# Denominators on two scratch tiles, key work from GpSimd to VectorE and ScalarE, and chunks of 256, 256 and seven times 512 tokens

## The chip, the core and the metric

The kernel runs on one core of a Trainium2 chip. The metric is the time of one execution in microseconds (us), taken on the device. The core's engines work side by side, each through its own queue in the order of the program, and wait for one another through semaphores: TensorE (PE in the rows; PEld is its loading of weights) multiplies, VectorE (DVE) and ScalarE (ACT) work on single elements, GpSimd (POOL) does the same more slowly, and SyncE (SP) issues transfers. SBUF is the core's memory for operands, PSUM the one that TensorE writes.

## What is computed

The first half is attention with random features, for 8 batches of 576 tokens and 8 heads of 64 dimensions, 128 features (M). The second half is a layer of 512 to 2048 and back to 512 columns on all 4608 tokens:

```python
def phi(x):                       # x is q or k, scaled
    proj = np.einsum('bhsd,md->bhsm', x, omega)
    sq = np.sum(x * x, axis=-1, keepdims=True) / 2.0
    h = proj - sq
    h = h - np.max(h, axis=-1, keepdims=True)
    return np.exp(h) / np.sqrt(m)
q_p, k_p = (phi(q_s), phi(k_s))
kv = np.einsum('bhsm,bhsd->bhmd', k_p, v)
z = np.sum(k_p, axis=2)
num = np.einsum('bhsm,bhmd->bhsd', q_p, kv)
den = np.einsum('bhsm,bhm->bhs', q_p, z)[..., None] + 1e-06
attn = num / den
# x: attn with heads side by side, (4608, 512)
h = x @ w_in
out = (h - np.tanh(h)) @ w_out
```

## The kernel before

The products run in a rounded 32-bit format (F32R). To keep the precision of 32 bits, an operand is split into a high part (the rounded value) and a low part (the rest), and two or three products take the place of one.

The tokens are cut into chunks of `SIZE = [256, 256, 256, 384, 384, 512, ...]` (chunks 0 and 1 are worked as one of 512). The program has two lists of steps. `ORDER` is the start: it decodes the weights, and does the keys of batches 0 to 2 and the queries of chunks 0 and 1. `LATER` holds all the rest, written as tokens `unit.step.slot`, and each engine's queue gets its instructions in just this order. Units are:

- `k` + batch + pair of heads (`k_unit`): the keys. Steps `p`, `c`, `t`, `e` make the features (project, copy out of PSUM, row minimum, exponential) for five groups of tokens, A0, A1, M, B0 and B1; head A has groups A0 and A1, head B has B0 and B1, and M is the last 64 tokens of either head, one head on partitions 0 to 63 and the other on 64 to 127. `kh`/`kl` split the features (`khl`), `vh`/`vl` the values (`vhl`), `kv` multiplies them into `pk`. `zA`, `zB`, `zM` sum the features over tokens into `zs`, `zh`/`zl` split the sum, and `ca` to `wv` turn and split the result, `kvw`, with `zb` the sum spread over all partitions.
- `q` + chunk + pair (`q_unit`): the queries. The same steps `p` to `e` for each tile of 128 tokens, then `d` (denominators: for each tile, head and batch one `tensor_tensor_reduce` on DVE, whose product goes to a scratch tile `junk` and whose sum goes to `dn`), `n` (reciprocal and division), `z`, `a`, `l` (turn and split), `m` (numerators), `ta`, `tv`, `xh`, `xl` (into the layer's input).
- `f` + chunk + slice of 128 columns of the 2048 (`f_unit`): the layer. `h0`, `h1` are 12 products on TensorE, `th` is tanh on ScalarE, `g` a subtraction on DVE (line 759), `gh` (ScalarE) and `gl` (DVE) the split, `o0` to `o3` the products with `w_out`. A unit of a chunk of 256 tokens takes two slices at once and is 512 columns wide on DVE and ScalarE, one of a chunk of 384 is 384 wide. `s` units copy out and send.

In a key unit GpSimd does the low parts of the features (line 646), the high parts of the values (659, with zeros set for group M at 656 and 657), the sums (680, 681, 685, 686) and the low part of `zs` (693). DVE does the rest of the element work beside ScalarE. Group M's values are split on 64 partitions at a time, one operation for each head (664).

Of the kernel before, what the change touches and what calls it, by code (L numbers as in the profile page):

```python
# [89 lines left out]
s0.c2.1 f21.h0.6 s0.c3.0 s0.d2 q30.n1 s0.d3 q31.t0 f21.h1 q31.t1 q31.e0 q31.t2 q31.e1 q32.sv q30.z0.0 q31.e2 k30.pA0.4  # L90
k30.pA1.7 q31.d0 f21.th q33.ld f20.o0.2 q30.a0 q31.d1 k30.cA0.0 k30.cA1 f21.g f20.o1.3 q30.l0 f21.gh q31.d2 k30.pM.0
f21.gl f22.h0.6 k30.cM.0 q31.n0 q31.n1 f22.h1 k30.tA0 k30.tA1 k30.eA0 k30.tM k30.vlA1 k30.eA1 q30.m0.4 k30.khA0.0
f21.o0 f22.th k30.klA0 k30.khA1.1 q30.ta0.2 f22.g k30.klA1 k30.eM f21.o1 q30.tv0 f22.gh k30.zA.0 f22.gl q30.z1.7
f23.h0.6 q30.a1 q30.l1 f23.h1 q30.m1.0 f23.th q32.p0.4 q32.p1.7 q30.ta1 f23.g f22.o0 q32.c0.0 q32.c1 q30.tv1 f23.gh
q32.t0 f22.o1 f23.gl q32.e0 q32.t1 q32.d0 q32.e1 q31.z0.0 q32.p2.4 q31.a0 q32.d1 k30.pB0.7 f24.h0.6 q32.c2 q33.sa
q31.l0 q32.t2 k30.cB0.0 q33.sv f24.h1 q32.e2 q32.d2 q40.ld q31.m0.0 q32.n0 f24.th k30.pB1.4 f23.o0 q31.ta0.3 q32.n1
k30.cB1 f24.g k31.sa q31.tv0 f23.o1 k30.tB0 f24.gh k30.tB1 k30.eB0 f24.gl q31.z1.0 k30.eB1 k30.kvA0.7 k31.sv0 k30.kvA1
q31.a1 k30.vhM.0 q33.p0.4 k30.khM.0 f25.h0.6 k30.khB0.1 q33.c0.1 q31.l1 k30.klM q33.t0 k30.klB0 k30.vlM q33.e0 f25.h1
k31.sv1 k30.zB.0 q33.d0 k32.ld q31.m1.0 f25.th k30.zM q33.p1.4 k30.kvM q31.ta1 f25.g f24.o0 q33.c1 k30.vhB0.0 q31.tv1
f25.gh k30.vhB1.1 q33.t1 f24.o1 f25.gl q33.e1 k30.khB1.0 q33.d1 k30.klB1 q32.z0.0 k30.vlB0 q33.p2.4 k30.vlB1 q32.a0  # L100
f26.h0.6 k31.lv q33.c2 q32.l0 q40.sa q33.t2 f26.h1 q33.e2 q40.sv q33.d2 q41.ld q32.m0.0 f26.th q33.n0 k30.kvB0 k30.kvB1
q32.ta0.1 k31.vhA0.0 q32.z1.4 f26.g k30.ca.0 f25.o0 k31.vhA1.1 q32.a1 q32.tv0 f26.gh q32.l1 f26.gl f25.o1 q33.n1
k30.zh.0 k30.cv q32.m1.0 k30.zl k31.vlA0 q40.p0.4 k31.vlA1 q32.ta1 f27.h0.6 q40.c0.0 q32.tv1 q40.t0 f27.h1 q40.e0
q30.xh q40.d0 q31.xh q33.z0.0 q30.xl f27.th q40.p1.4 q31.xl k30.kt q32.xh f27.g f26.o0 q33.a0 q40.c1 q32.xl f27.gh
q33.l0 k30.ka k30.zb f26.o1 f27.gl q40.t1 k30.kb q40.e1 q33.m0.0 q40.p2.4 k30.wa q40.d1 k31.pA0.7 q33.ta0.0 f30.h0.6
q40.c2 q33.tv0 q41.sa q40.t2 q33.z1.0 k31.cA0.0 k30.wv q41.sv k31.pA1.4 q40.e2 q33.a1 q40.d2 k31.cA1 q42.ld q33.l1
q40.n0 q41.p0.0 q40.n1 q41.c0.1 q41.t0 k31.tA0 q41.e0 q33.m1.0 k31.tA1 q41.p1.7 k31.eA0 q41.d0 q40.z0.4 q33.ta1
k31.khA0.0 q40.a0 q33.tv1 k31.klA0 q41.c1 q40.l0 k31.eA1 q41.p2.0 q41.t1 q33.xh k31.pM.4 k31.zA.0 k31.khA1.1 q41.e1
k31.kvA0.7 q33.xl q41.c2 q41.d1 q42.sa k31.klA1 f30.h1 q41.t2 k31.cM.0 k31.vhM.0 q42.sv q41.e2 k31.pB0.0 f30.th
# [1037 lines left out]
```

## Time and profile before

| | |
|---|---|
| median of 3 runs | 1060.26 us (1058.77 to 1066.28) |
| profiled execution | 1063.08 us, of which the span is 1061.3 |
| PE busy in the span | 1029.4 us (97%) |
| DVE busy | 796.7 us (75%) |
| ACT busy | 651.7 us (61%) |
| POOL busy | 267.3 us (25%) |

The span goes from the first to the last instruction. Busy time is the union of an engine's instructions. PE's ends are modelled, since its products are pipelined, so that a busy PE can still be a waiting one, and its pace is better read from the distance between starts. A clock of 1.00 is 2.4 GHz, 0.50 is 1.2 GHz.

### The profile page before, as it was taken

How to read it: one execution, taken by the hardware profiler on the slowest of the kernel's cores; microseconds unless marked ns; L12 is line 12 of the kernel's file. 1: busy time of each engine (PE TensorE's matmuls, PEld its weight loads, DVE VectorE, ACT ScalarE, POOL GpSimd, SP SyncE). 2: the span in 40 equal slices, each digit the busy share in tenths (PEclk: the TensorE clock that was granted, in tenths of full speed). 3: DMA queues.
4: the chain of work that ended last, by engine and by line, in shares of the span. 5: the costliest groups of instructions: out<-in, count | busy, mean ns of one | idle time of the engine just before them, and what ended most of it. 6: DMA issues, size and time to landing. Idle time of an engine off the chain costs nothing.

```text
span 1061.3 us, 17049 instructions
## 1 busy us (share of the span) xinstructions
PE 1029.4 (97%) x5500; PEld 866.5 (82%) x5500; DVE 796.7 (75%) x2624; ACT 651.7 (61%) x1565; POOL 267.3 (25%) x477
## 2 busy tenths in 40 slices
PE   9999999989999999999999999999999999999998
PEld 8788767878888888888788878877888888888886
DVE  4989857899997998999889988898668637523222
ACT  6997666676766676777576756675556436423222
POOL 1333420313143226333542255215500000000000
PEclk8999999989999999999999999999999999999999
DMA  6888872001011101211120111101010001001001
GB/s 216 254 228 240 218 177 74 20 27 61 21 33 64 32 22 45 63 33 27 40 74 23 32 44 62 33 21 33 12 50 21 11 1 40 1 1 40 1 1 40
DMA packets 27929, 64.60 MB, mean 61 GB/s; under 512 B 3008, under 2 KB 5952, under 8 KB 27840
## 3 DMA queue, kind: packets, MB, share of 16 engines
q1 hardware_dynamic: 20368, 37.65, 11.5%
q10 hardware_dynamic: 5168, 17.47, 5.0%
q0 software_dynamic: 2304, 8.39, 4.3%
q8 instruction: 44, 0.72, 0.3%
q14 instruction: 45, 0.37, 0.1%
HBM read 45.67 MB, written 9.44 MB: 52 GB/s over the span
## 4 chain that ended last, share of the span: by engine, by line
PE 63%; DVE 20%; ACT 9%; issue 4%; POOL 2%; DMA 2%; ACTq 0%; DVEq 0%; SPq 0%; POOLq 0%
PE h L519 26%; PE po L542 8%; PE po L544 8%; PE po L543 8%; DVE zf L573 2%; PE pj_q L432 2%; DVE zf L759 2%; PE pt L586 2%; PE pk L673 1%; DVE phi_q L581 1%; DVE zr L761 1%; DMA raw<-w 1%; PE k_pj L835 1%; PE k_pk L858 1%; DVE ql L594 1%
## 5 line engine op out<-in xcount | busy, mean ns | idle before, releaser
L519 PE MATMUL h<-xa,w 128*128 128x512 f32 (+2 forms) x1920 | 423.2, 370 | 4.3 <-DVE zf L759 3.4
L519 PEld LDWEIGHTS h<-xa,w 128*128 128x128 f32 x1920 | 339.6, 189 | 59.0 <-DVE zf L759 4.8
L542 PE MATMUL po<-w,zr 128*128 128x512 f32 x544 | 216.3, 398 | 2.5 <-ACT zr L532 2.5
L544 PE MATMUL po<-w,zr 128*128 128x512 f32 x544 | 213.3, 392 | 0.0
L543 PE MATMUL po<-w,zr 128*128 128x512 f32 x544 | 212.9, 391 | 0.0
L758 ACT ACTIVATE zf<-h 128x512 f32<-128x512 f32 (+1 forms) x138 | 78.5, 569 | 194.3 <-PE h L519 190.0
L759 DVE TENSOR_TENSOR zf<-h,zf 128x512 f32<-128x512 f32 (+1 forms) x138 | 90.6, 657 | 133.8 <-ACT zf L758 132.9
L760 ACT CAST zr<-zf 128x512 fp32r<-128x512 f32 (+1 forms) x138 | 82.4, 597 | 67.6 <-DVE zf L759 66.0
L544 PEld LDWEIGHTS po<-w,zr 128*128 128x128 f32 x544 | 102.2, 188 | 23.2 <-DVE zr L534 0.9
L542 PEld LDWEIGHTS po<-w,zr 128*128 128x128 f32 x544 | 102.6, 189 | 18.8 <-ACT zr L532 3.2
L543 PEld LDWEIGHTS po<-w,zr 128*128 128x128 f32 x544 | 102.5, 188 | 15.4
L761 DVE TENSOR_TENSOR zr<-zf,zr 128x512 fp32r<-128x512 f32 (+1 forms) x138 | 94.7, 686 | 26.9 <-ACT zr L760 25.0
L449 ACT ACTIVATE phi_q<-phi_q,nb_q 128x128 f32<-128x128 f32 x240 | 79.6, 396 | 22.3 <-DVE nb_q L443 21.1
L573 DVE CUSTOM_DVE_ANT_0 zf<-phi_q,zb 128x128 f32<-128x128 f32 (+1 forms) x200 | 63.4, 317 | 16.4 <-DVE dn L573 1.0
L646 POOL TENSOR_TENSOR khl_A<-phi_kA,khl_A 128x256 fp32r<-128x256 f32 x40 | 30.9, 773 | 146.4 <-DVE khl_A L642 144.9
L443 DVE CUSTOM_DVE_ANT_0 phi_q<-pj_q,phi_q 128x128 f32<-128x128 f32 x240 | 57.3, 285 | 5.0 <-ACT phi_q L438 4.3
L432 PE MATMUL pj_q<-om,qx 128*128 128x256 f32 x240 | 47.1, 300 | 6.2 <-DVE ql L594 2.1
L438 ACT COPY phi_q<-pj_q 128x256 f32<-128x256 f32 x120 | 41.2, 374 | 13.6 <-PE pj_q L432 12.9
L432 PEld LDWEIGHTS pj_q<-om,qx 128*128 128x128 f32 x240 | 37.1, 191 | 14.6 <-DVE ql L594 2.9
L594 DVE TENSOR_TENSOR ql<-pt,qh 128x512 fp32r<-128x512 f32 (+1 forms) x64 | 41.7, 652 | 3.9 <-ACT qh L590 3.2
L449 ACT ACTIVATE phi_kA<-phi_kA,nb_k_A 128x128 f32<-128x128 f32 x80 | 26.7, 393 | 24.1 <-DVE nb_k_A L443 23.9
L581 DVE TENSOR_TENSOR phi_q<-phi_q,dn 128x512 f32<-128x512 f32 (+1 forms) x64 | 40.5, 666 | 1.1
(181 smaller groups left out, 1708.9 us busy)
## 6 DMA issues: line engine op xcount, KB each, us to landing
raw<-w ACTq DMA_DIRECT2D x32, 512.0 KB, 5.3
w<-a POOLq DMA_DIRECT2D x16, 512.0 KB, 6.5
qf<-qT SPq DMA_DIRECT2D x24, 256.0 KB, 2.7
kf<-kT SPq DMA_DIRECT2D x20, 288.0 KB, 2.9
v<-vt SPq DMA_DIRECT2D x20, 288.0 KB, 2.8
out<-xs SPq DMA_DIRECT2D x18, 256.0 KB, 2.0
out<-zf SPq DMA_DIRECT2D x17, 256.0 KB, 2.2
k_v<-va SPq DMA_DIRECT2D x12, 330.0 KB, 4.2
```

What stands on the lines that cost most here:

```text
L432: nc.tensor.matmul(w["pj"][:, i], x, om2, start=True, stop=True)
L443: nc.vector.tensor_tensor_reduce(u[kind][:, at + i], w["pj"][:, i, :M], u[kind][:, at + i], scale=-SCALE, scalar=3.0e38, op0=ALU.add, op1= ...
L449: nc.scalar.activation(u[kind][:, at + i], u[kind][:, at + i], AF.Exp, bias=w["nb"][:, i : i + 1], scale=-1.0)
L519: nc.tensor.matmul(o, w_, x, start=i == 0, stop=i == len(prods) - 1)
L542: nc.tensor.matmul(po[t], gh[:, 2 * j + t], wt[f][:, 0, DM:], start=first, stop=False)
L543: nc.tensor.matmul(po[t], gh[:, 2 * j + t], wt[f][:, 1, DM:], start=False, stop=False)
L544: nc.tensor.matmul(po[t], gl[:, 2 * j + t], wt[f][:, 0, DM:], start=False, stop=last)
L573: nc.vector.tensor_tensor_reduce(junk[r], u["ph"][r, i], kvs[b, c][1][r, h], scale=1.0, scalar=EPS, op0=ALU.mult, op1=ALU.add, accum_out=u ...
L758: th=lambda: nc.scalar.activation(g, blocks(u["p"])[:, 0:n], AF.Tanh),
L759: g=lambda: nc.vector.tensor_sub(g, blocks(u["p"])[:, 0:n], g),
L760: gh=lambda: nc.scalar.copy(gh, g),
L761: gl=lambda: nc.vector.tensor_sub(gl, g, gh.bitcast(F32)))
```

## The change

- The denominators write their products to two scratch tiles in turns, one for each head, and the loop runs over batches outside and heads inside. The reciprocal becomes a step `r` of its own.
- All of GpSimd's operations in `k_unit` go: the low parts of the features, the sums and the low part of `zs` to DVE, the high parts of the values to ScalarE. `zA`, `zB` and `zM` are each split into two steps that can be placed apart.
- The values come from the host with ten blocks of 128 tokens in place of nine: group M has a block for each head, with zeros on the other head's partitions, so that no zeros are set and M's values are split like the others'.
- `SIZE` becomes `[256, 256, 256, 256, 512, ...]`: chunk 3 has 256 tokens and chunk 4 512. The products of the layer keep their columns.
- `PLACES` takes every tag's place once in a set order before the first step, which sets addresses alone.
- `LATER` is written anew.

```diff
-SIZE = [256, 256, 256, 384, 384, 512, 512, 512, 512, 512, 512]
+SIZE = [256, 256, 256, 256, 512, 512, 512, 512, 512, 512, 512]
...
+    junks = [zf[:, 13], zf[:, 14]]
...
-            for h in range(2):
-                i = 2 * t + h
-                for b, s, e in pieces:
-                    s, e = max(s, t * P), min(e, (t + 1) * P)
+            for b, s, e in pieces:
+                s, e = max(s, t * P), min(e, (t + 1) * P)
+                for h in range(2):
+                    i = 2 * t + h
                     if s < e:
                         r = slice(s - t * P, e - t * P)
                         nc.vector.tensor_tensor_reduce(
-                            junk[r], u["ph"][r, i], kvs[b, c][1][r, h], scale=1.0, scalar=EPS,
+                            junks[h][r], u["ph"][r, i], kvs[b, c][1][r, h], scale=1.0, scalar=EPS,
                             op0=ALU.mult, op1=ALU.add, accum_out=u["dn"][r, i : i + 1])
+        def recip():
+            nc.vector.reciprocal(u["dn"], u["dn"])
...
-            nc.gpsimd.tensor_sub(k[:, :m, 1], u["ph" + g[0]][:, t : t + m], k[:, :m, 0].bitcast(F32))
+            nc.vector.tensor_sub(k[:, :m, 1], u["ph" + g[0]][:, t : t + m], k[:, :m, 0].bitcast(F32))
...
-            if g == "M":
-                nc.gpsimd.memset(v[0:D, 1].bitcast(F32), 0.0)
-                nc.gpsimd.memset(v[D:P, 0].bitcast(F32), 0.0)
-            for p, i, j in parts(g, t0):
-                nc.gpsimd.tensor_copy(v[p, i, 0], u["v"][p, j])
+            nc.scalar.copy(v[:, :, 0], u["v"][:, v0 : v0 + 2])
...
-            for p, i, j in parts(g, t0):
-                nc.vector.tensor_sub(v[p, i, 1], u["v"][p, j], v[p, i, 0].bitcast(F32))
+            nc.vector.tensor_sub(v[:, :, 1], u["v"][:, v0 : v0 + 2], v[:, :, 0].bitcast(F32))
...
-            zt = ak.tile([P, 2, M], F32, tag="c1", name=f"zt_{n}_{h}")
-            nc.gpsimd.tensor_add(zt, ph[:, 0:2], ph[:, 2:4])
-            nc.gpsimd.tensor_add(zs[:, h], zt[:, 0], zt[:, 1])
-        def z_mid():
-            pm = u["phM"]
-            nc.gpsimd.tensor_add(zs[0:D, 0], zs[0:D, 0], pm[0:D, 0])
-            nc.gpsimd.tensor_add(zs[D:P, 1], zs[D:P, 1], pm[D:P, 0])
+            u["zt", h] = ak.tile([P, 2, M], F32, tag="c1", name=f"zt_{n}_{h}")
+            nc.vector.tensor_add(u["zt", h], ph[:, 0:2], ph[:, 2:4])
+        def zsum2(h):
+            nc.vector.tensor_add(zs[:, h], u["zt", h][:, 0], u["zt", h][:, 1])
+        def z_mid(h):
+            r = slice(D * h, D * h + D)
+            nc.vector.tensor_add(zs[r, h], zs[r, h], u["phM"][r, 0])
...
-            nc.gpsimd.tensor_sub(u["zhl"][:, 1], zs, u["zhl"][:, 0].bitcast(F32))
+            nc.vector.tensor_sub(u["zhl"][:, 1], zs, u["zhl"][:, 0].bitcast(F32))
...
+    mid = np.zeros((B - 2, NC, 2, P, D), v.dtype)
+    for h in range(2):
+        mid[:, :, h, D * h : D * h + D] = vt[:, :, 4, D * h : D * h + D]
+    vt = np.concatenate([vt[:, :, :4], mid, vt[:, :, 5:]], axis=2).transpose(0, 1, 3, 2, 4)
```

Two places show what stands in the queues now. The first is the unit of queries of chunk 5, pair 1, on DVE before. The rows with `zf,dn` are denominators (`zf` holds the scratch), each followed by the reading of its sum into `dn`; between them stand the casts of the keys' high parts (`khl`) and the features of keys and queries:

```order
L642 CAST khl_1_B_5953<-phi_kB_1_5925 128x2x128 [waits Activation_49]
L573 ISA zf,dn_1_5882<-phi_q_1_5833,zb_1_4814 128x128 [waits Activation_49]
L573 ISA dn_1_5882 128x1
L573 ISA zf,dn_1_5882<-phi_q_1_5833,zb_1_4814 128x128 [waits DVE_49,Activation_49]
L573 ISA dn_1_5882 128x1
L443 ISA phi_kB_1_5925,nb_k_1_B_5975<-pj_k_1_B_5946,phi_kB_1_5925 128x128 [waits Activation_49]
L443 ISA nb_k_1_B_5975 128x1
```

The same unit's denominators of two token tiles on DVE after the change, four in a row:

```order
L579 ISA zf,dn_1_5922<-phi_q_1_5857,zb_1_4825 128x128 [waits Activation_49]
L579 ISA dn_1_5922 128x1
L579 ISA zf,dn_1_5922<-phi_q_1_5857,zb_1_4825 128x128 [waits Activation_49]
L579 ISA dn_1_5922 128x1
L579 ISA zf,dn_1_5922<-phi_q_1_5857,zb_1_4825 128x128 [waits DVE_49,Activation_49]
L579 ISA dn_1_5922 128x1
L579 ISA zf,dn_1_5922<-phi_q_1_5857,zb_1_4825 128x128 [waits DVE_49,Activation_49]
L579 ISA dn_1_5922 128x1
```

The second denominator no longer waits for the first; the third and the fourth wait for the one two before.

The second place is the end of the key unit of batch 5, pair 1. On GpSimd before, from the zeros of group M to the sums of the middle:

```order
L656 MEMSET vhl_1_M 64x128 [waits PE_49]
L657 MEMSET vhl_1_M 64x128 [waits Pool_49]
L659 CAST vhl_1_M<-v_1_5677 64x64 x2
L646 TENSOR_TENSOR khl_1_M<-phi_km_1_5820,khl_1_M 128x128 [waits DVE_49,Activation_49,Pool_49]
L659 CAST vhl_1_B_5932<-v_1_5677 128x2x64 [waits PE_49]
L659 CAST vhl_1_B_5958<-v_1_5677 128x2x64 [waits DVE_49,PE_49]
L646 TENSOR_TENSOR khl_1_B_5953<-phi_kB_1_5925,khl_1_B_5953 128x2x128 [waits DVE_49]
L680 TENSOR_TENSOR zt_1_1_5995<-phi_kB_1_5925 128x256 [waits Activation_49]
L681 TENSOR_TENSOR zs<-zt_1_1_5995 128x128 [waits Pool_49]
L646 TENSOR_TENSOR khl_1_B_5998<-phi_kB_1_5925,khl_1_B_5998 128x2x128 [waits DVE_49]
L685 TENSOR_TENSOR zs<-zs,phi_km_1_5820 64x128
L686 TENSOR_TENSOR zs<-zs,phi_km_1_5820 64x128 [waits Pool_49]
```

The same work on DVE after the change, with the layer's `gl` (line 760 now) and a query's or key's input among it:

```order
L760 TENSOR_TENSOR zr<-zf,zr 128x512 [waits Activation_49]
L649 CAST khl_1_B_5989<-phi_kB_1_5933 128x2x128 [waits DVE_49,PE_49,Activation_49]
L649 CAST khl_1_B_5993<-phi_kB_1_5933 128x2x128 [waits Activation_49]
L653 TENSOR_TENSOR khl_1_B_5989<-phi_kB_1_5933,khl_1_B_5989 128x2x128 [waits DVE_49]
L653 TENSOR_TENSOR khl_1_B_5993<-phi_kB_1_5933,khl_1_B_5993 128x2x128 [waits DVE_49]
L677 TENSOR_TENSOR zt_1_1_6008<-phi_kB_1_5933 128x256
L661 TENSOR_TENSOR vhl_1_B_5991<-v_1_5740,vhl_1_B_5991 128x2x64 [waits Activation_49]
L680 TENSOR_TENSOR zs<-zt_1_1_6008 128x128 [waits DVE_49]
```

The low parts stand two places behind their high parts on the same engine, and the sum `zs` two behind `zt`; the values' high parts (`vhl`) now come from ScalarE.

## Rows read from the trace of the kernel before

**Rows 1.** The page's slices: busy tenths of 40.
```profile
DVE  4989857899997998999889988898668637523222
POOL 1333420313143226333542255215500000000000
```
**Rows 2.** Windows: length, busy (count) of PE, PEld, DVE, ACT, POOL, clock, DMA.
```profile
174.90:774.10 599.20, 580.27 (x3077) 493.90 (x3077) 527.06 (x1916) 404.80 (x1030) 215.72 (x398) 0.99 0.13 38
774.10:1061.30 287.20, 283.18 (x1308) 235.13 (x1306) 137.05 (x373) 113.77 (x228) 0.00 (x0) 1.00 0.06 19
```
**Rows 3.** Windows of four layer units each, of the 22 in the middle.
```profile
202.40:242.10 39.70, 35.79 (x200) 30.53 (x199) 36.54 (x143) 28.04 (x74) 12.90 (x25) 0.87 0.09 26
...
749.00:774.10 25.10, 25.10 (x127) 21.21 (x126) 15.41 (x48) 12.53 (x32) 13.01 (x24) 1.00 0.01 2
```
**Rows 4.** Timeline of PE, two stretches: start us, us, engine, line, operation, names, shapes, count.
```profile
940.16 2.88 PE L519 MATMUL h<-xa,w 128*128 128x512 f32 x12
942.88 0.39 PE L542 MATMUL po<-w,zr 128*128 128x512 f32 x1
...
341.81 1.20 PE L519 MATMUL h<-xa,w 128*128 128x384 f32 x6
342.85 0.25 PE L600 MATMUL pn<-qh,k_kvw 128*128 128x192 f32 x1
...
343.37 0.64 PE L432 MATMUL pj_q<-om,qx 128*128 128x256 f32 x4
343.85 0.40 PE L542 MATMUL po<-w,zr 128*128 128x512 f32 x1
```
**Rows 5.** Timeline of DVE: a cast, a subtraction and the instruction behind them.
```profile
489.62 0.28 DVE L642 CAST khl_A<-phi_kA 128x256 fp32r<-128x256 f32 x1
489.82 0.68 DVE L761 TENSOR_TENSOR zr<-zf,zr 128x512 fp32r<-128x512 f32 x1
490.42 0.28 DVE L443 CUSTOM_DVE_ANT_0 phi_kA<-pj_k_A,phi_kA 128x128 f32<-128x128 f32 x1
```
**Rows 6.** Timeline of DVE, denominators of one unit of queries.
```profile
485.38 0.28 DVE L573 CUSTOM_DVE_ANT_0 zf<-phi_q,zb 64x128 f32<-64x128 f32 x1
...
485.70 0.29 DVE L573 CUSTOM_DVE_ANT_0 zf<-phi_q,zb 64x128 f32<-64x128 f32 x1
...
486.79 0.29 DVE L573 CUSTOM_DVE_ANT_0 zf<-phi_q,zb 128x128 f32<-128x128 f32 x1
...
487.24 0.29 DVE L573 CUSTOM_DVE_ANT_0 zf<-phi_q,zb 128x128 f32<-128x128 f32 x1
```
**Rows 7.** Timeline of DVE, denominators of the early stage, on two scratch tiles.
```profile
47.62 0.29 DVE L932 CUSTOM_DVE_ANT_0 junk<-zf,k_zb 128x128 f32<-128x128 f32 x1
...
47.84 0.29 DVE L932 CUSTOM_DVE_ANT_0 zf<-q_phi,k_zb 128x128 f32<-128x128 f32 x1
```
**Rows 8.** Timelines of DVE and POOL at one time.
```profile
497.87 0.85 DVE L573 CUSTOM_DVE_ANT_0 zf<-phi_q,zb 128x128 f32<-128x128 f32 x1
...
497.83 0.74 POOL L646 TENSOR_TENSOR khl_B<-phi_kB,khl_B 128x256 fp32r<-128x256 f32 x1
```
**Rows 9.** Groups by line of DVE, the middle: count, busy us, mean ns, idle before.
```profile
L573 DVE CUSTOM_DVE_ANT_0 zf<-phi_q,zb 128x128 f32<-128x128 f32 x116 | 38.0, 328 | 10.1 <-ACT phi_q L449 0.5 <-DVE dn L573 0.5
L443 DVE CUSTOM_DVE_ANT_0 phi_kB<-pj_k_B,phi_kB 128x128 f32<-128x128 f32 x80 | 18.7, 283 | 1.0 <-ACT phi_kB L438 0.9
L642 DVE CAST khl_B<-phi_kB 128x256 fp32r<-128x256 f32 x40 | 17.2, 434 | 2.9 <-PE pk L673 1.7 <-ACT phi_kB L449 0.3 <-POOL vhl_B L659 0.2
L700 DVE TENSOR_TENSOR c<-pk,c 128x256 f32<-128x256 f32 x20 | 8.3, 416 | 1.4 <-ACT c L697 1.3
```
**Rows 10.** Timeline of PE at the longest wait of the middle.
```profile
231.99 0.69 PE L432 MATMUL pj_q<-om,qx 128*128 128x256 f32 x2 [2.05 <-DVE ql L594]
```
**Rows 11.** A group by line of ACT, whole span; and GpSimd's wait for slots.
```profile
L718 ACT CAST kvw<-zf 128x128 fp32r<-128x128 f32 x20 | 5.9, 297 | 7.3 <-DVE zf L738 7.3
...
POOL vhl_M L656 <- PE pk L673: 79.9, 10, 18.0
```

More of the change, by code (lines that the diff above doesn't have):

```diff
@@ L90 @@
[L90 to L109, printed above, removed]
@@ L629, in lv @@
         def lv():
-            u["v"] = ak.tile([P, 9, D], F32, tag="vr", name=f"v_{n}")
+            u["v"] = ak.tile([P, 10, D], F32, tag="vr", name=f"v_{n}")
             nc.sync.dma_start(u["v"], vt[b - 2, c])
@@ L645, in key_lo, with val_hi, val_lo @@
             k = u["k" + g]
-            nc.gpsimd.tensor_sub(k[:, :m, 1], u["ph" + g[0]][:, t : t + m], k[:, :m, 0].bitcast(F32))
-        def parts(g, t0):
-            if g != "M":
-                return [(slice(0, P), slice(0, 2), slice(t0, t0 + 2))]
-            return [(slice(D * h, D * h + D), h, t0) for h in range(2)]
-        def val_hi(slot, g, t0):
-            v = u["v" + g] = ak.tile([P, 2, 2, D], F32R, tag=f"vhl{slot}", name=f"vhl_{n}_{g}")
-            if g == "M":
-                nc.gpsimd.memset(v[0:D, 1].bitcast(F32), 0.0)
-                nc.gpsimd.memset(v[D:P, 0].bitcast(F32), 0.0)
-            for p, i, j in parts(g, t0):
-                nc.gpsimd.tensor_copy(v[p, i, 0], u["v"][p, j])
-        def val_lo(g, t0):
+            nc.vector.tensor_sub(k[:, :m, 1], u["ph" + g[0]][:, t : t + m], k[:, :m, 0].bitcast(F32))
+        def val_hi(slot, g, v0):
+            v = u["v" + g] = ak.tile([P, 2, 2, D], F32R, tag=f"vhl{slot}", name=f"vhl_{n}_{g}")
+            nc.scalar.copy(v[:, :, 0], u["v"][:, v0 : v0 + 2])
+        def val_lo(g, v0):
             v = u["v" + g]
-            for p, i, j in parts(g, t0):
-                nc.vector.tensor_sub(v[p, i, 1], u["v"][p, j], v[p, i, 0].bitcast(F32))
+            nc.vector.tensor_sub(v[:, :, 1], u["v"][:, v0 : v0 + 2], v[:, :, 0].bitcast(F32))
         def kv(*slot, g):
@@ L723, in w_lo @@
             kvs[b, c][0] = w.rearrange("p a d -> p (a d)")
-        for g, t0, m in (("A0", 0, 2), ("A1", 2, 2), ("M", 4, 1), ("B0", 5, 2), ("B1", 7, 2)):
+        for v0, (g, t0, m) in zip(range(0, 10, 2), (("A0", 0, 2), ("A1", 2, 2), ("M", 4, 1), ("B0", 5, 2), ("B1", 7, 2))):
             lhs = lambda t0=t0, m=m: [u["x"].rearrange("p h s -> p (h s)")[:, t * P : (t + 1) * P] for t in range(t0, t0 + m)]
@@ L1103, in favor_attention_ffn @@
         zsum_tile.append(ak.tile([P, 2, M], F32, name="zs"))
+        for tag, kb, dtype in PLACES:
+            ak.tile([P, int(kb * 256)], dtype, tag=tag, name=f"place_{tag}")
         issue(LATER, dict(k=k_unit, q=q_unit, f=f_unit, s=s_unit, x=x2_unit))
```

520 lines of the change are left out of this document (272 added, 248 removed).

## Prediction

> **What bounds the kernel now.** I read the page's slices first: GpSimd works up to the 29th of 40 slices and not after it, and VectorE (DVE) stands at seven to nine tenths from the 7th to the 28th and then falls [rows 1]. So there are three stretches, cut at the first `g` step of a layer unit of chunk 2 (174.9 us) and of chunk 8 (774.1): a start that the change leaves alone, a middle of 599.2 us in which GpSimd is busy for 215.7, and an end of 287.2 us without GpSimd, where DVE is half idle [rows 2].
>
> TensorE's own work follows from the distance of starts: 12 products of 512 columns take 2.72 us, so 0.227 each, 6 of 384 columns 1.04 us, so 0.173, and 4 of the projection 0.48, so 0.12 [rows 4]. The middle has 1,545 products of 512 columns (351 us), 384 of 384 (66), 168 of 256 at the projection's 0.12 (20), and some 1,000 of the attention at 0.03 to 0.23 (118): 555 us. The trace has 599, so TensorE loses 44 there. The end, priced so, is 286 of 287: nothing is lost. The middle is the whole question.
>
> DVE in the middle: busy 527 us [rows 2], 16 more in pauses before denominators (L573; 10.1 of them before the form in [rows 9]), and some 9 in pauses of 0.03 that come wherever two instructions use different partitions. That is 552 of 599. DVE is thus as full as TensorE's 555, but unevenly. From 202.4 to 242.1 it is busy 36.5 of 39.7 us while TensorE's own work is 30.6; from 749.0 on it is busy 15.4 of 25.1 [rows 3]. In the first of these TensorE waits 2.05 us at 231.99 for a DVE result (`ql`, L594) [rows 10], and right behind it the granted clock is at the lower level, 1.2 GHz, for a while (0.87 over the window) [rows 3].
>
> So I cut the middle into pieces of four layer units (22 pieces), and took for each the larger of TensorE's work and DVE's occupied time. The sum is 578 us; the trace has 599. What is left, 21 us, is about 1 us a piece (from -0.3 to 2.4): waits of one in-order engine for another inside a piece. That rule, larger of the two plus 1 us, is what I carry to the change.
>
> **The change part by part: DVE.** Prices are distances of starts, since an instruction's last 0.085 us lies under the next one's start: 256 columns with one input 0.20, 512 columns 0.60 [rows 5]. For 256 columns with two inputs L700 shows 0.416 long [rows 9], so 0.33; 128 columns of two inputs are 0.20 by the same step. An instruction on half the partitions starts 0.03 after its predecessor's end and delays its successor alike: two such denominators stand 0.32 apart [rows 6], so an isolated one costs 0.44 in all.
>
> Added from GpSimd, over the 20 key units of the middle: low parts of keys 80 x 0.33 + 20 x 0.20 = 31; sums `zt` 40 x 0.33 = 13; `zs` 40 x 0.20 = 8; middle sums on half the partitions 40 x 0.44 = 17; `zhl` low 20 x 0.33 = 7. Together 76 us.
>
> Removed: (1) *Denominators.* Two that write the same scratch stand 0.45 apart, because the second waits for the first (487.24 against 486.79) [rows 6]; in the early stage, where the same operation writes two tiles in turns, the distance is 0.22 [rows 7]. The built order has 140 denominators that wait on the one directly before, some 110 of them in the middle; after the change, none. 110 x 0.23 = 25. (2) *Last values.* Two 64x64 operations with pauses (0.62 in all) become one of 0.20: 20 x 0.42 = 8. (3) *Shapes.* Chunks 3 and 4 take 24 units of 512 columns through DVE instead of 32 of 384: 2 x 32 x 0.47 - 2 x 24 x 0.60 = 1, plus some 2 on the queries. (4) *GpSimd beside DVE.* A denominator of 0.29 takes 0.85 while GpSimd's `khl_B` (0.74 long) runs over it [rows 8]. The cast of the keys (0.29 undisturbed, [rows 5]) has a mean of 434 ns over 40, denominators 328 over 116, while L443, with one input in PSUM, keeps 283 [rows 9]. Summed over all forms, time above the undisturbed length is 44 us, of which keys' casts 14, denominators 8, values 10. With GpSimd idle in the middle I take all 44 as gone.
>
> The Trainium skill, SBUF — State Buffer, section Who interferes with whom, says that a DVE instruction with two SBUF inputs, or in a two-port mode, and a GpSimd instruction that reads SBUF exclude each other for a whole instruction; by that rule the lengthening ends with GpSimd's work, and the rows, L443's above all, agree.
>
> Sum for DVE: 552 + 76 - 25 - 8 - 3 - 44 = 548 us. On balance DVE gains 4 us; the time must come from evenness.
>
> **The change: the rest.** ScalarE takes 100 casts of values at some 0.21 (L718's cast of that size is 0.297 long [rows 11], less the overlap), 21 us. In the middle ScalarE is busy 405 of 599 [rows 2], so I cost them at nothing; a piece has at most 24 us of ScalarE in 28, and without that cover they would be 21 us. A cast that waits for its slot (two tiles, freed by L673) holds up ScalarE's queue, with `tanh` behind it; before, GpSimd waited there 80 us in all at no cost [rows 11]. TensorE: products of the same columns in chunks 3 and 4, so 557 for 555. The loads of values grow from 288 to 320 KB on SP's queue and stay far ahead of use. The reciprocal becomes a step of its own and the reserved places only fix addresses: neither has a price. GpSimd's wait chains (high part on DVE, low part on GpSimd, product on TensorE) lose two crossings of engines.
>
> I counted the built order of the change by these prices, in 20 pieces of four units (TensorE / DVE): chunk 2: 26.4/26.1, 26.1/22.4; chunk 3: 31.2/26.9, 28.5/30.1; chunk 4: 28.8/28.8, 28.6/28.3, 27.8/28.8, 26.0/25.9; chunk 5: 29.0/28.7, 29.2/29.1, 27.8/29.5, 25.5/25.6; chunk 6: 29.8/30.1, 29.8/30.1, 26.5/26.9, 26.2/26.3; chunk 7: 29.1/27.1, 29.9/30.0, 25.9/25.1, 25.0/16.9. DVE sums to 543 (548 above). The glut of the first pieces is gone, and nowhere does DVE exceed TensorE by 2 us. The larger ones sum to 562.5, against 578 before. With 1 us a piece the middle is 582.5: 16.7 less than 599.2.
>
> The profiled execution took 1063.1 us (span 1061.3, and 1.8 around it), 2.8 above the median of the three runs, 1060.3 (1058.8 to 1066.3). So 1046.4 for a profile, and **1044** for the median.
>
> **Bounds.** The unseen price is the 1 us a piece, now that DVE has no slack for 11 pieces in a row. Below: 0.3 (the low third of the pieces before), middle 568.5. Above: 2.4, the worst piece, in every piece: 610. I take 1, nearest to the pieces of before in which both were within 1.5 us (0.5 to 2.4, mean 1.05).
>
> **Rivals.**
> *Waits melt too.* With GpSimd out of the chains, 0.3 a piece: 568.5, so 30.7 less: 1030. For it: TensorE's products of keys (L673) wait for GpSimd's `khl` here and there. Against it: most waits name DVE or ScalarE. Chance 0.17.
> *Given back.* DVE and TensorE are both at 100%, so any DVE idling is lost: 2 us a piece, 602: 1063, no change. For it: DVE idled 47 us of the middle for other engines even though it was the fuller one in places. Chance 0.22.
> *Own results (the other side).* DVE now waits for itself: a low part needs the high part just cast, and a wait like the denominator's costs 0.23. If all 240 moved operations paid, 55 us: 1099. It undoes the gain from 73 of them on, and makes the kernel 1% slower from 119. The built order puts 18 directly behind what they need, most others two apart, where 0.03 remains. Chance 0.06.
> *Offload undone.* If the stretched rows don't come from GpSimd, the 44 us stay: DVE 592 over TensorE's 557, middle 612, 1073. The Trainium skill, Perfetto Trace Analysis, section Optimizing Scalar/DVE Operations, advises moving work off a saturated DVE, even to GpSimd, which is this rival's direction (it adds that moving between those two might not help). [rows 8] speaks against. Chance 0.05.
> The forecast itself has 0.50, own range 1036 to 1052.
>
> **Numbers.** A measurement here tells about 1% (10.6 us) from no change. Faster by more: 0.17, and most of the 0.50 (0.43): 0.60. Within: the rest and nearly all of 0.22, so 0.29. Slower: 0.11. The range 1030 to 1063 reaches from the first rival to the second and leaves out the last two and tails, under 2 in 10.
>
> **What would show it.** Right: no GpSimd work past chunk 1; keys' casts at 0.29 and denominators 0.22 apart; the middle near 582 with DVE occupied over 540 of it; no 2 us wait near 230 and no lower clock behind it. Wrong: casts still at 0.43 (offload undone); DVE gaps in front of low parts (own results); TensorE waiting for `zf`, `ql` or `zr` all through chunks 4 to 6 (given back); ScalarE idle before value casts with `tanh` late behind them.

## The result, and the profile after

The change makes the kernel 3.5% faster: 1023.77 us as the median of 4 executions (1022.21 to 1025.07), against 1059.76 for the kernel before beside it; the ratio is 0.9654, with a 95% interval of 0.9613 to 0.9695. The prediction was 1044, with a range of 1030 to 1063: the right direction, but less than half of the gain, and the time lies below the range.

The page's slices of the kernel after, busy tenths of 40 and the granted clock in tenths, answer to [rows 1]:

```profile
DVE  5999768979999999999999999999698248324222
POOL 1334320000000000000000000000000000000000
PEclk9999999999999999999999999999999999999999
```

GpSimd ends with the start, VectorE is at nine tenths or more from the 10th slice to the 28th with no dip, and the clock never falls. Windows cut at the same steps as in [rows 2], with the same columns (length, busy and count of PE, PEld, DVE, ACT, POOL, clock, DMA share, GB/s):

```profile
0.00:170.10 170.10, 162.58 (x1117) 134.35 (x1118) 134.62 (x353) 133.25 (x314) 49.42 (x77) 1.00 0.76 211
170.10:736.40 566.30, 565.97 (x3097) 485.25 (x3096) 528.85 (x2109) 418.83 (x1111) 0.00 (x0) 1.00 0.14 42
736.40:1023.30 286.90, 282.80 (x1306) 234.74 (x1304) 133.67 (x371) 112.40 (x225) 0.00 (x0) 1.00 0.06 19
```

The middle went from 599.2 to 566.3 us: 32.9 of the 38.0 us between the two profiled spans (1061.3 and 1023.3). The end is the same (287.2 and 286.9). The start is 4.8 shorter, but that is no effect that could be read: over the traces below it lies between 167 and 178.5 us, 166.9 to 170.1 where the granted clock in it is 1.00 and 172.7 to 178.5 where it is 0.93 to 0.98 (0.98 before, 1.00 after). So kernels are compared by medians and by their middles, each from one profiled execution; between the runs below and the kernel after, the two comparisons agree within some 2 us, but for e4 (7). TensorE is busy for all but 0.33 us of the middle, and in the groups by line the whole span's products of the layer had 1.0 us of idle time ahead of them, which is that of the start; the waits of [rows 10] are gone (the view of TensorE's waits in the middle is empty):

```profile
L525 PE MATMUL h<-xa,w 128*128 128x512 f32 (+1 forms) x1920 | 432.7, 370 | 1.0 <-DVE zf L536 1.0
```

Two windows of four layer units, the places of [rows 3]: units 4 to 7 of chunk 2, and the last four of chunk 7. The first had 36.5 us of VectorE in 39.7 before, at a clock of 0.87; now:

```profile
196.80:223.40 26.60, 26.55 (x176) 24.24 (x176) 22.29 (x94) 18.10 (x47) 0.00 (x0) 1.00 0.12 32
711.10:736.40 25.30, 25.20 (x120) 20.80 (x119) 16.90 (x59) 13.70 (x38) 0.00 (x0) 1.00 0.00 1
```

The single prices came out as counted. Timeline of DVE (start us, length us): a cast of keys and its low part 0.33 behind, and two denominators 0.21 apart where [rows 6] had 0.45:

```profile
403.45 0.29 DVE L649 CAST khl_B<-phi_kB 128x256 fp32r<-128x256 f32 x1 [0.35 <-ACT phi_kB L455]
403.78 0.43 DVE L653 TENSOR_TENSOR khl_B<-phi_kB,khl_B 128x256 fp32r<-128x256 f32 x1
...
411.13 0.28 DVE L579 CUSTOM_DVE_ANT_0 zf<-phi_q,zb 128x128 f32<-128x128 f32 x1
...
411.34 0.28 DVE L579 CUSTOM_DVE_ANT_0 zf<-phi_q,zb 128x128 f32<-128x128 f32 x1
```

Groups by line of DVE in the middle (count, busy us, mean ns, idle before), which answer to [rows 9]: casts 288 ns for 434, denominators 286 for 328 and with 0.7 us of pauses ahead for 10.1.

```profile
L579 DVE CUSTOM_DVE_ANT_0 zf<-phi_q,zb 128x128 f32<-128x128 f32 x116 | 28.5, 286 | 0.7 <-ACT phi_q L455 0.6
...
L649 DVE CAST khl_B<-phi_kB 128x256 fp32r<-128x256 f32 x40 | 11.1, 288 | 2.1 <-ACT phi_kB L455 1.4 <-PE pk L670 0.3
```

So these parts came out near the prices of the prediction, and still 16 us more were gained in the middle than it said. The question for the experiments was where these came from.

### The profile page after: what moved, and what is told of

Its sections match the earlier page's. It is cut to its first block, busy times and chain, and to the rows that moved or that the text cites. A ratio compares the mean times of both kernels' runs of the same rounds, so it can differ in the third digit from the quotient of the medians.

```text
span 1023.3 us, 16763 instructions
## 1 busy us (share of the span) xinstructions
PE 1011.4 (99%) x5516; PEld 854.3 (83%) x5516; DVE 797.1 (78%) x2829; ACT 664.5 (65%) x1648; POOL 49.4 (5%) x77
## 4 chain that ended last, share of the span: by engine, by line
PE 86%; DVE 6%; ACT 3%; DMA 2%; issue 2%; POOL 0%; ACTq 0%; POOLq 0%; DVEq 0%; SPq 0%
PE h L525 35%; PE po L548 11%; PE po L550 11%; PE po L549 11%; PE pj_q L438 3%; PE pt L593 3%; PE pk L670 2%; PE pn L608 1%; PE pn L607 1%; DMA raw<-w 1%; PE k_pk L857 1%; PE pj_k_B L438 1%; PE pj_k_A L438 1%; DMA k_v<-va 1%; PE k_pj L834 1%
## 5 line engine op out<-in xcount | busy, mean ns | idle before, releaser
L525 PE MATMUL h<-xa,w 128*128 128x512 f32 (+1 forms) x1920 | 432.7, 370 | 1.0 <-DVE zf L536 1.0
L525 PEld LDWEIGHTS h<-xa,w 128*128 128x128 f32 x1920 | 330.2, 188 | 56.9 <-DVE zf L536 1.2
L758 DVE TENSOR_TENSOR zf<-h,zf 128x512 f32<-128x512 f32 x130 | 89.6, 689 | 130.1 <-ACT zf L757 129.0
L757 ACT ACTIVATE zf<-h 128x512 f32<-128x512 f32 x130 | 77.3, 595 | 163.9 <-PE h L525 161.1
L549 PEld LDWEIGHTS po<-w,zr 128*128 128x128 f32 x544 | 102.4, 188 | 15.7
L760 DVE TENSOR_TENSOR zr<-zf,zr 128x512 fp32r<-128x512 f32 x130 | 89.5, 688 | 25.0 <-ACT zr L759 24.0
L759 ACT CAST zr<-zf 128x512 fp32r<-128x512 f32 x130 | 80.9, 622 | 38.1 <-DVE zf L758 36.9
L449 DVE CUSTOM_DVE_ANT_0 phi_q<-pj_q,phi_q 128x128 f32<-128x128 f32 x240 | 57.8, 284 | 1.9 <-ACT phi_q L444 1.6
L579 DVE CUSTOM_DVE_ANT_0 zf<-phi_q,zb 128x128 f32<-128x128 f32 (+1 forms) x200 | 49.8, 286 | 1.1 <-ACT phi_q L455 0.6
L444 ACT COPY phi_q<-pj_q 128x256 f32<-128x256 f32 x120 | 41.8, 371 | 12.0 <-PE pj_q L438 11.7
L597 ACT CAST qh<-pt 128x512 fp32r<-128x512 f32 (+1 forms) x64 | 35.6, 556 | 12.2 <-PE pt L593 11.5
L593 PE MATMUL pt<-zf,phi_q 128*128 128x128 f32 x240 | 36.8, 273 | 0.1
```

What stands on the lines that cost most here:

```text
L449: nc.vector.tensor_tensor_reduce(u[kind][:, at + i], w["pj"][:, i, :M], u[kind][:, at + i], scale=-SCALE, scalar=3.0e38, op0=ALU.add, op1= ...
L525: nc.tensor.matmul(o, w_, x, start=i == 0, stop=i == len(prods) - 1)
L549: nc.tensor.matmul(po[t], gh[:, 2 * j + t], wt[f][:, 1, DM:], start=False, stop=False)
L593: nc.tensor.transpose(u["pt", h][:, t * P : (t + 1) * P], u["ph"][:, 2 * t + h], ident)
L757: th=lambda: nc.scalar.activation(g, blocks(u["p"])[:, 0:n], AF.Tanh),
L758: g=lambda: nc.vector.tensor_sub(g, blocks(u["p"])[:, 0:n], g),
```

## The experiments

The prediction's rule counts, for each piece of four layer units, the larger of TensorE's and VectorE's own time. What the middle takes beyond the sum of the larger ones is called *the rest* here: 21 us before, of which the prediction kept 20 (1 us a piece); after, 566.3 less 562.5, so 3.8. The table counts all runs in this way. VectorE's own time takes the prices of the prediction on the instructions in their order, plus *stretching*: the time by which its instructions in that run's own trace are longer than undisturbed ones (44 us before, 0.0 after).

| kernel | median us | middle us | larger ones, sum | rest | stretching |
|---|---|---|---|---|---|
| before | 1059.8 | 599.2 | 578.2 | 21.0 | 44 |
| after | 1023.8 | 566.3 | 562.5 | 3.8 | 0 |
| e1: old list, two tiles | 1049.2 | 589.7 | 567.9 | 21.8 | 46 |
| e2: old list, on DVE and ACT | 1053.5 | 595.6 | 574.0 | 21.6 | 0 |
| e3: new list, on GpSimd | 1035.5 | 577.2 | 557.3 | 19.9 | 42 |
| e4: new list, one tile | 1046.6 | 581.9 | 581.8 | 0.1 | 0 |
| e5: new list, sums on GpSimd | 1033.9 | 577.6 | 559.6 | 18.0 | 31 |
| e6: GpSimd reads beside it | 1069.3 | 612.8 | 608.3 | 4.5 | 52 |
| e7: GpSimd writes beside it | 1029.5 | 572.0 | 567.7 | 4.3 | 7 |
| e8: 14.4 us more on DVE | 1032.9 | 576.0 | 573.1 | 2.9 | 0 |
| e9: 116 steps shifted | 1058.6 | 602.3 | 562.5 | 39.8 | 0 |
| e10: casts on ACT | 1034.3 | 576.4 | 557.5 | 18.9 | 0 |
| e11: 65 steps earlier | 1050.7 | 593.4 | 562.5 | 30.9 | 0 |
| e12: 56 steps later | 1034.6 | 577.3 | 562.5 | 14.8 | 0 |

These sums rest on counted prices. Counted with each trace's own times instead (VectorE busy and in pauses of up to 0.15 us, TensorE by its distances of starts), the rest is 23 to 24 us before and in e1 and e2, 7 after, 9 to 12 in e4, e6, e7 and e8, 18 to 22 in e3, e5 and e10, and 40 in e9. The groups keep their order, but the new list with its own sharing of the work has some rest left.

**One part at a time.** The first four runs set the list of steps (`LATER`, always with its chunk sizes) against the rest of the change.

```diff
+    junks = [zf[:, 13], zf[:, 14]]
...
-                            junk[r], u["ph"][r, i], kvs[b, c][1][r, h], scale=1.0, scalar=EPS,
+                            junks[h][r], u["ph"][r, i], kvs[b, c][1][r, h], scale=1.0, scalar=EPS,
```

> The kernel before with one edit: denominators write to two scratch tiles in turns; the old list of steps and GpSimd's work stay. In the middle VectorE loses about 22 us of its own waits, but only in pieces where it is the fuller engine does that count: the sum of the larger of TensorE and VectorE over the 22 pieces falls by some 6 us. Three theories on the 21 us that lay above that sum in the kernel before and 4 us after. GpSimd theory (its stretching of VectorE and its steps inside the chains made them) and list theory (the old order of steps made them): only the 6 us go, about 1054. Denominator theory (those waits delayed what stood behind them): the 21 us melt too, about 1035.

Measured: 1049.2, a ratio of 0.9914 (0.9878 to 0.995) to the kernel before, the middle 9.5 us shorter. The sum of the larger ones falls by 10.3 (with this run's stretching), a little more than the 6 that were expected, and the rest stays at 21.8. The denominators' waits did not make it.

The second run is the kernel after with the old list and its chunks (the new half-steps of the sums put in):

```diff
-SIZE = [256, 256, 256, 256, 512, 512, 512, 512, 512, 512, 512]
+SIZE = [256, 256, 256, 384, 384, 512, 512, 512, 512, 512, 512]
...
-LATER = (the list of the kernel after)
+LATER = (the list of the kernel before, zA2, zB2, zM2 one VectorE step behind zA, zB, zM, and r ahead of n0)
```

> The old list of steps and the old chunks, but all other parts of the change: key work on VectorE and ScalarE in place of GpSimd, two scratch tiles, values by zeros. The second halves of the split sums stand one VectorE step behind the first. Counted as in the prediction VectorE has 554 us in the middle, TensorE 557, and the larger ones of 22 pieces sum to 574. GpSimd theory: 4 us above that as in the kernel after, middle 578, about 1038. List theory: the old list keeps its 21 us, middle 595, about 1055.

Measured: 1053.5, 0.9953 (0.9918 to 0.9989), the middle 595.6. That is what the list theory said (1055 and 595), and not the GpSimd theory's 1038. With the old list, taking all work from GpSimd makes the middle 5.9 us longer than the run before, although the stretching goes from 46 us to 0.0. TensorE waits here as in the kernel before, 18.3 us of visible waits in the middle of either (waits of PE: for what, us in total, times, longest; the first three rows):

```profile
PE pk L676 <- DVE khl_B L659: 3.0, 5, 1.1
PE pj_q L444 <- DVE ql L607: 2.4, 3, 1.8
PE pj_q L444 <- DVE nb_q L455: 2.1, 3, 1.6
```

The second of these includes a wait of 1.8 us, at the place where [rows 10] showed one of 2.05. Behind it the clock is again at the lower level for a while, 0.91 over that window of 39.1 us, which costs about 3.5 of the 21.6 (0.09 of 39.1):

```profile
193.70:232.80 39.10, 35.02 (x203) 30.26 (x202) 36.95 (x154) 30.28 (x83) 0.00 (x0) 0.91 0.10 29
```

The third run takes the new list and gives the key work back to GpSimd:

```diff
-            nc.vector.tensor_sub(k[:, :m, 1], u["ph" + g[0]][:, t : t + m], k[:, :m, 0].bitcast(F32))
+            nc.gpsimd.tensor_sub(k[:, :m, 1], u["ph" + g[0]][:, t : t + m], k[:, :m, 0].bitcast(F32))
...
-            nc.scalar.copy(v[:, :, 0], u["v"][:, v0 : v0 + 2])
+            nc.gpsimd.tensor_copy(v[:, :, 0], u["v"][:, v0 : v0 + 2])
...
(zt, zs, the middle sums and the low part of zhl in the same way)
```

> The new list, chunks, two scratch tiles and values by zeros, but the key work (low parts, sums, high parts of values) back on GpSimd. VectorE's own work is then 464 us undisturbed, 508 with the 44 us of stretching seen before; TensorE's 557 is the larger nearly everywhere. List theory: 4 us above the sum, middle 562, about 1019, not slower than the kernel after. GpSimd theory: about 1 us or more a piece, middle 577 or more, 1035 or more, since GpSimd's slow steps (0.4 to 0.8 us each, in its own queue) stand in the chains again and stretch VectorE.

Measured: 1035.5, so 11.7 more than the kernel after, as the GpSimd theory said. VectorE has 79 us less of its own work here, and 42 of stretching, and TensorE's sum is the larger one almost everywhere; yet the rest is 19.9. So neither theory holds alone: the old list has its 21 us with or without GpSimd, and the new list gets 20 when its steps run on another engine. Against the same two tiles with the old list (e1, 589.7) the new list, with its chunks and the values' blocks of zeros, brings 12.5 us of the middle while GpSimd keeps its work, and 29.3 without it (e2 to the kernel after). VectorE stands for GpSimd's sums, though longer in total for ScalarE's tanh (15.0 us), and TensorE stands for GpSimd's low parts (waits in the middle):

```profile
DVE zhl L688 <- POOL zs L684: 6.3, 6, 2.3
...
PE pk L670 <- POOL khl_B L653: 2.8, 5, 0.9
```

The fourth undoes the two tiles in the new list:

```diff
-    junks = [zf[:, 13], zf[:, 14]]
+    junks = [zf[:, 13], zf[:, 13]]
```

> The kernel after with one edit undone: both heads' denominators write to the same scratch tile, in the new list. The denominators now stand next to each other, so VectorE pays 26 us of own waits more in the middle: 569 against TensorE's 557, and the larger ones sum to 582. GpSimd and list theories: 4 us above that, middle 586, about 1043. Denominator theory: about 1 us a piece comes back as well, middle 602, about 1059. If VectorE still has slack that the count does not see, below 1035.

Measured: 1046.6, middle 581.9 for the 582 to 586 that were expected. Of the 26 us of own waits that were counted the trace has 19 (VectorE busy and in pauses: 558 for 539 in the kernel after), and these cost 15.6. The larger-of sum is met to 0.1, but in part because it counts too much: 569 us of VectorE for the trace's 558, while VectorE also stood 20.3 us for ScalarE, in 38 waits. What holds is that VectorE is the fuller engine in most pieces here and sets the pace. The middle's window, and the denominators (0.7 us of pauses ahead of them after the change):

```profile
167.40:749.20 581.80, 575.34 (x3095) 484.40 (x3095) 536.58 (x2108) 421.36 (x1110) 0.00 (x0) 1.00 0.14 41
...
L579 DVE CUSTOM_DVE_ANT_0 zf<-phi_q,zb 128x128 f32<-128x128 f32 x116 | 33.6, 289 | 8.0 <-ACT phi_q L455 0.6
```

**GpSimd's share.** Is it the stretching or the waits for GpSimd's results? In the next run GpSimd has the sums alone, which nobody needs at once:

```diff
-            nc.vector.tensor_add(u["zt", h], ph[:, 0:2], ph[:, 2:4])
+            nc.gpsimd.tensor_add(u["zt", h], ph[:, 0:2], ph[:, 2:4])
...
(zs, the middle sums and the low part of zhl in the same way)
```

> The kernel after with the sums zt, zs, the middle sums and the low part of zhl back on GpSimd; low parts of keys and high parts of values stay on VectorE and ScalarE. VectorE loses 45 us of work in the middle and gets back some 17 us of stretching (84 us of GpSimd work at 42 us per 200 us, as in run e3). Chain theory: the 11 us by which run e3 was longer than the kernel after in the middle came from TensorE waiting for GpSimd's low parts of keys; the sums are not waited for at once, so 562 to 566 and about 1020 to 1024. Stretching theory: they came from VectorE's lengthened instructions; 17 of 42 us of it bring 4 to 5 us, about 1028.

Measured: 1033.9, as much as with all the work on GpSimd. The chain theory falls: VectorE waited 0.3 us in all for GpSimd, and TensorE and ScalarE show no wait for it. That leaves stretching, but it is not shown to be the cause: the middle is 11.3 us longer for 30.7 of stretching, well above the price that was expected, while VectorE's own work is some 40 us less, and e10 below is nearly as much longer (10.1) with no stretching at all. The stretching falls for the most part on the keys' casts and low parts (groups of DVE by line, middle). TensorE's products of keys take longer, 30.5 us from start to start for the 200 at L670 in place of 25.6, summed over the middle; but they do so in e9 too (30.6), where nothing is stretched.

```profile
L649 DVE CAST khl_B<-phi_kB 128x256 fp32r<-128x256 f32 x40 | 17.5, 445 | 2.3 <-ACT phi_kB L455 1.6 <-PE pk L670 0.3
L653 DVE TENSOR_TENSOR khl_B<-phi_kB,khl_B 128x256 fp32r<-128x256 f32 x40 | 21.8, 556 | 0.4
```

Two runs then put GpSimd beside the kernel after with work that nobody needs; they differ in one line:

```diff
+        def side(source, p=P, cols=256):
+            if source is not None:
+                nc.gpsimd.tensor_copy(scr[:, 256:257], source)
+            u["s"] = 0
+            o = scr[0:p, u["s"] : u["s"] + cols]
+            nc.gpsimd.tensor_sub(o, om2[0:p, 0:cols].bitcast(F32), om2[0:p, 0:cols].bitcast(F32))
...
(the other run: nc.gpsimd.memset(o, 0.0); called beside the low parts, zt, zs, the middle sums and the low part of zhl)
```

> The kernel after, and beside it GpSimd runs 220 subtractions and as many one-column copies that nobody needs: 128x256 or smaller, both inputs the constant om in SBUF, output a scratch of its own, started beside the same steps where the kernel before had its work; nobody waits for GpSimd's results. Some 150 us of GpSimd work. Stretching theory: VectorE's instructions lengthen by about 31 us (44 per 216 as before), VectorE 574 in the middle, larger ones 584, about 1041 to 1045. If lengthening did not matter and only the waits for GpSimd's results did: 1024 to 1028.

> As the run before, but each subtraction is a memset of the same size, which reads nothing. If VectorE lengthens because both engines read SBUF, VectorE's stretching falls to a few us (the one-column copies still read) and the time stays at 1024 to 1028. If any GpSimd work beside it lengthens VectorE, the stretching is in proportion to GpSimd's busy time, as in the run before.

Measured: 1069.3 with reads, slower than the kernel before, although nobody waits for GpSimd: 51.9 us of stretching (31 expected, from some 150 us of GpSimd's work; it was busy for 198) make the middle 46.5 longer. With writes 1029.5, a little above the 1024 to 1028 that were expected if reads alone counted: 7.2 us of stretching, 5.7 of middle. Here, where the list and the sharing of all needed work are those of the kernel after, stretching costs 0.8 to 0.9 us per us. What is stretched by what is seen in single rows. With reads, the timelines of DVE and POOL show a low part of 0.42 that takes 0.86 behind a subtraction of GpSimd that began 0.04 earlier:

```profile
417.14 0.86 DVE L662 TENSOR_TENSOR khl_B<-phi_kB,khl_B 128x256 fp32r<-128x256 f32 x1
...
417.10 0.61 POOL L654 TENSOR_TENSOR scr<-om 128x256 f32<-128x256 f32 x1
```

With writes, the low part keeps 0.42 over a memset (404.61 over 404.54), but the cast of 0.29, which has one input, takes 0.52 (408.07 over 408.13); all 7.2 us of stretching in that run are such casts:

```profile
404.61 0.42 DVE L662 TENSOR_TENSOR khl_B<-phi_kB,khl_B 128x256 fp32r<-128x256 f32 x1
408.07 0.52 DVE L658 CAST khl_B<-phi_kB 128x256 fp32r<-128x256 f32 x1
...
404.54 0.31 POOL L654 MEMSET scr<- 128x256 f32 x1
...
408.13 0.60 POOL L654 MEMSET scr<- 128x256 f32 x2
```

The Trainium skill, SBUF — State Buffer, section Who interferes with whom, says this: a VectorE instruction with two SBUF inputs contends with a GpSimd instruction that reads SBUF and not with one that only writes, while casts and copies in a two-port mode contend with GpSimd. The rows agree, but for GpSimd's copies of one column, which read SBUF too and lengthened nothing that can be seen (last section).

**VectorE's room.** A small dose of work that nobody needs:

```diff
+        def sub_g():
+            nc.vector.tensor_sub(g, blocks(u["p"])[:, 0:n], g)
+            if 3 <= ch <= 7:
+                nc.vector.tensor_copy(ak.tile([P, 256], F32, tag="scr", name=f"scr_{ch}_{s}"), om2.bitcast(F32))
```

> The kernel after with 72 additional casts-free copies of 128x256 on VectorE (0.20 us each, 14.4 us), one behind each layer unit's subtraction in chunks 3 to 7, into a scratch that nobody reads. Larger-of rule: VectorE 557 in the middle, the larger ones sum to 573, with the 2 to 4 us above it 575 to 577, about 1033 to 1035. If VectorE still has room (it stood idle for some 24 of 566 us), below 1027. If every microsecond is lost, 1038.

Measured: 1032.9, middle 576.0: the larger-of rule with 2.9 us above it. Two thirds of what VectorE gets more are lost, although it stands idle for 26 us of the middle in the kernel after.

**Where single steps stand.** So the rest is neither GpSimd alone nor a full VectorE. What is left is the order of single steps. In the next run 116 of the 288 steps `th`, `g`, `gh` and `gl` of chunks 3 to 7 stand one step earlier or later in the queue of their engine. An example of a move to an earlier place, in the list:

```diff
-q62.e1 k43.vlA1 f52.gl q61.z1.7
+q62.e1 f52.gl k43.vlA1 q61.z1.7
```

> The kernel after, with 116 of the 288 steps th, g, gh and gl of the layer units in chunks 3 to 7 moved by one step of the same engine's queue, earlier or later by lot; nothing else is changed, the same work on the same engines. VectorE's and TensorE's sums per piece stay as they are, so by evenness over pieces alone the time stays within 2 us of the kernel after: 1022 to 1026. Fine-order theory: what lies above the larger-of sum (21 us with the old list on either engine, 4 with the new one) comes from where single steps stand; with two steps in five out of place by one, a good part of the 17 us returns, 1030 to 1040.

Measured: 1058.6, no different from the kernel before (0.9973 to 1.0023). The middle is 36 us longer, with the same work on the same engines (the same counts, and busy times within 4 us but for TensorE's, which can hold waits) and with the same counted sums per piece. The waits of TensorE in the middle are back, 20 us of them, nearly all for results of the attention (the window of the middle, and the first three rows of waits):

```profile
168.64:770.99 602.34, 581.10 (x3097) 485.53 (x3096) 532.52 (x2108) 421.16 (x1111) 0.00 (x0) 1.00 0.13 40
...
PE pk L673 <- DVE khl_B L656: 5.3, 8, 1.1
PE pt L596 <- DVE nb_q L452: 1.4, 2, 0.8
PE pj_q L441 <- DVE nb_k_B L452: 1.3, 1, 1.3
```

> Of the shifts of run e9 (+36 us in the middle) only those to an earlier place: 65 steps th, g, gh, gl of the layer stand one step earlier in their queue, so that a step of the attention behind them comes 0.6 us later. In e9 TensorE waited for attention results (khl, nb_q, nb_k, ql, c) and hardly for the layer's. If the attention's steps are the ones without room, these moves hold nearly all of the 36 us: 1050 or more. If every misplaced step costs the same 0.31 us, 65 of them give 20 us: 1044.

> The other half of run e9: 56 steps th, g, gh, gl of the layer stand one step later in their queue, behind a step of the attention (0.2 to 0.4 us). If the attention's steps are the ones without room, the layer's results have room enough and this costs little: 1024 to 1030. If every misplaced step costs the same 0.31 us, 56 of them give 17 us: 1041.

Measured: 1050.7 with the 65 earlier steps, 1034.6 with the 56 later ones; the middles are 27.1 and 11.0 us longer, 0.42 and 0.20 us a step. They are 38 together where the common run had 36; but e9 has only 60 of the 65 earlier steps, and the five more account for the 2. So a layer's step that is put ahead of one of the attention costs twice as much as the reverse, but the latter isn't free either: both theories are half right. The two moves are not of one size, though. By an estimate from the distances of starts in the trace of the kernel after, an earlier move delays the attention's step by 0.56 us on average (the layer's step), a later one the layer's step by 0.40 (the attention's). Per us of delay that is 0.75 and 0.49, so the attention's steps are the dearer ones per us too, by half. One more run gives the keys' casts to ScalarE in the same list:

```diff
-            nc.vector.tensor_copy(u["k" + g][:, :m, 0], u["ph" + g[0]][:, t : t + m])
+            nc.scalar.copy(u["k" + g][:, :m, 0], u["ph" + g[0]][:, t : t + m])
```

> The kernel after with the casts of the keys' high parts on ScalarE in place of VectorE: 100 instructions, 18 us off VectorE in the middle, some 23 us more on ScalarE (busy 419 of 566 before that). Larger-of rule: VectorE 524 against TensorE's 557, the larger ones 557.5, with 4 us above it 561, about 1019. ScalarE theory: the casts stand in ScalarE's queue between tanh and the exponentials and the list was not made for it, so waits grow and eat the gain: 1024 or more.

Measured: 1034.3, 10.5 us slower, as the ScalarE theory said, though VectorE has 18 us less to do and ScalarE has room (447 of 576 us busy). VectorE now stands for the casts, in the row of the waits with the most time (behind the window of the middle):

```profile
178.52:754.89 576.37, 571.82 (x3097) 484.91 (x3096) 516.15 (x2009) 446.94 (x1210) 0.00 (x0) 1.00 0.14 41
...
DVE khl_B L653 <- ACT khl_B L649: 12.1, 18, 1.4
```

The shifts and this run point the same way: the new list is good for just this sharing of the work over the engines. No run was faster than the kernel after.

## Why the direction was right and the size wrong

**What bounds it.** Right: TensorE in the end, TensorE and VectorE together in the middle. The end and TensorE's own 557 us stayed.

**VectorE's sum.** Right. 543 to 548 us were forecast. The trace has 529 busy, 8 in pauses of about 0.03 and 3 in short ones, so 540. The stretching went from 44 to 0 as taken, the denominators are 0.21 apart, and with the moved operations the sum is near. One term was too large: the denominators' 25 us are 19 by the trace of e4. The two tiles alone are worth 10.0 us with the old list (e1: 1049.2 against 1059.2 beside it) and some 23 with the new one (e4 by the medians; in the profiled executions 15.6 in the middle and 5.3 behind it). The move of GpSimd's work to VectorE and ScalarE is worth nothing by itself: with the old list it costs 5.9 us of the middle, with the new one it brings 10.9.

**The larger ones.** Right: 562.5 for 578, so 15.7 of the 32.9 us. The pieces follow the counted table: the longest of chunk 3 was counted at 31.2 and took 32.3, the one where VectorE was to lead by 1.7 (chunk 5, third) was counted at 29.5 and took 29.1.

**The step that failed** is the term "With 1 us a piece the middle is 582.5". It should have been 3.8 us over all 20 pieces, 0.19 a piece (some 7 us, or 0.35, with the trace's own times). I took the 1 us to be what two full in-order engines lose to each other, and chose it since the fullest pieces of before had it. It is no such constant. It goes with the list of steps and with the engine that each step runs on: 21 to 22 us in all three kernels with the old list, whatever the engines and tiles (before, e1, e2); nothing to 5 us (7 to 12 with the traces' own times) in the new list with its own sharing of the work, even with 7 to 52 us more on VectorE (e4, e6, e7, e8); 18 to 20 where steps of the new list run on other engines (e3, e5, e10); and 40 where 116 steps are out of place (e9). The term was 20 us and measured 3.8: these 16.2 us are what the middle gained beyond the forecast. They make 1044 into 1028; the last 4 us lie outside the middle and were not traced to a step (in the two profiled executions the start alone is 4.8 shorter, at a clock of 1.00 for 0.98).

That order alone, with the same work on the same engines, makes such a rest is shown by the shifts. I read the old list's 21 us as the same thing, a misfit between the order and the work, but that is argued: that they would go if the list were written anew for the kernel before was not tried. Longer steps by themselves make little of it (e6 stretches VectorE's by 52 us, and the rest is 4.5). Nor were the chunk sizes tried apart from the list. About 3.5 us of the old list's rest are the lower clock behind the longest wait (e2).

**Costed at nothing.** ScalarE's casts of values, 14 us more busy in the middle: right, TensorE waited for none of it. Loads of values, the step `r` and the places: nothing seen.

**The rivals.** *Waits melt too* named the size: 568.5 for the middle and 1030, near the 566.3 and 1023.8. Its reason, GpSimd out of the chains, holds only in part: run e2 has no GpSimd and keeps 21.6. So it met the size partly by luck. At 0.17 its chance was too low, and the range ended at its centre. *Given back*: wrong; no wait for `zf`, `ql` or `zr` is left. *Own results*: wrong; VectorE stands idle for 0.3 us in all ahead of the low parts, and the 16 of them directly behind their own cast start 0.02 after its end (the median). Its price of a denominator's wait, 0.23 us, was borne out by e4, where 74 stand 0.45 apart and about 0.8 of the 19 us reached the time. *Offload undone*: wrong; stretching is 0.0. The Trainium skill, Perfetto Trace Analysis, section Optimizing Scalar/DVE Operations, says that moving work off a full VectorE may make sense, with a caution about GpSimd. In the new list neither move helped: some 40 us of sums moved to GpSimd made the kernel 10 us slower (e5), and the casts moved to ScalarE 10.5 (e10).

**What would show it.** The four signs came: no GpSimd past chunk 1, casts at 0.29, denominators 0.22 apart, no 2 us wait near 230 and no lower clock. Only "the middle near 582" did not, and VectorE's "over 540" was met just about, with 540.

## What to carry to other kernels

Where a list of steps is written anew, what engines lose to each other under the old list says nothing of the new one: count the larger engine per piece, and let the range reach from no loss at all to the old loss, with good chances at either end. The order is itself worth tens of us here (36 of 1024 for 116 steps out of place by one), so that moving work between engines without fitting the order again can lose even where the engine that is relieved is nearly as full as the fullest. And time by which GpSimd stretches VectorE's instructions counted nearly in full where VectorE is as full as TensorE (e6, e7); with the old list, where the order had left a rest of 21 us, moving GpSimd's work, and with it 46 us of stretching, away gained nothing (e1 to e2).
